# Attention and a mixture of experts on one core: stores placed one by one, and a rewritten order of attention's instructions

## Chip, core and metric

One core of a Trainium2 chip runs the whole program. The metric is the device time of one execution in microseconds, as a median of several runs. The core has five instruction queues that run beside each other: PE (TensorE, matmuls), DVE (VectorE), ACT (ScalarE), POOL (GpSimd) and SP (SyncE, which here only issues DMAs). Each runs its own list strictly in order and waits on semaphores for the others.

## What is computed

Sliding-window attention with four sink positions, and after it a mixture of eight experts with top-2 routing on the attention's output rows.

```python
B, H, S, D = 4, 8, 768, 64          # attention: batches, heads, tokens, head width
n_sink, window = 4, 128
scores = (q @ k.T) / sqrt(D)
keep = (pos_k < n_sink) | (0 <= pos_q - pos_k < window)
a = softmax(where(keep, scores, -1e9)); attn = a @ v
x = attn.transpose(0, 2, 1, 3).reshape(3072, 512)
noisy = x @ w_gate + log1p(exp(x @ w_noise)) * noise      # 8 experts
top2, weights = two largest of noisy, softmax of the two
for e in range(8):
    for k in range(2):
        out[mask] += weight * (relu(x[mask] @ w1[e]) @ w2[e])   # 512 -> 1024 -> 512
```

## The kernel before

**Two phases.** Phase one does attention, the routing of three of the four batches, and the first gathers and weight loads of expert 0. Phase two does the routing of the last batch and the eight experts. Phase one works in 48 steps n: 16 pairs of heads g, three steps each, n = 3 g + jj, four pairs to a batch. A step goes through the engines like this (the names are those of the functions in `attention`):

- `qk` (PE): scores of 256 query rows, tile S in a PSUM bank "D"; in the trace L403.
- `prev` and `cur` (ACT or DVE, then DVE): masked copy into the buffer `cbuf`; `mins` (DVE): row maxima `mn`; `minus_max` (POOL): `nb`.
- `exps_sums` (ACT): eight instructions of the softmax's exponentials with their sums.
- `ptr` (PE): the probabilities transposed into a "D" bank (L493); for odd steps `pcopy` (POOL or ACT) first lays the sinks' columns into `pcbuf`.
- `ptr_c` (ACT or DVE) copies them to the tile CT, `ptr_m` (DVE or POOL) makes the masked copy CM, `sink_c` the tile ps.
- `pv` (PE): output in a bank "X" (L519 with CT, L522 with CM), for odd steps `sinks` (PE, L534); `pv_c` (ACT or DVE) copies it to xtn and `rows` (DVE) turns it into token rows in the tile xr.

There are three "D" banks and two of "X", shared by all of these, by the gate's projections (`logits`: L734, L742), by the routing's matmuls and by the transposes of gathered rows (L1087).

**Token rows through memory.** `rows_d` stores a step's rows of a batch (four heads' pairs together) from xr to the buffer x_rows in memory, as four DMAs of 128 KB in rows of 512 bytes. `routing` ends for a batch with `keep`, four DMAs of 36 KB that lay the gate weights behind the rows, in pieces of 48 bytes. `gather` fetches 128 rows for an expert by an indirect DMA that POOL issues, once the rows and the weights of its batch have landed; `norm` (DVE, L1079), a transpose on PE and two copies follow.

**What sets the order.** Every step is announced to a planner (`Plan.op`, `Plan.dma`) with an engine, an estimated duration and what it reads and writes. For phase one `Plan.replay` then emits the steps in exactly the sequence of the table ORDER; a digit of SIDE for each step that can go to either of two engines says which, and a digit of BANKS for each use of a bank says which bank. A DMA announced with `Plan.dma` takes two entries of ORDER, one on SP and one for its transfer. For phase two `Plan.run` makes a list schedule from the estimates. The estimates are compiled into the order and are no measurement; the program that runs has only the order and the semaphores.

**Dummy matmuls.** 32 matmuls on constants (`warm`, L363) stand between the first blocks of PE.

## Time and profile before

| | |
|---|---|
| time, median of 3 runs (lowest, highest) | 742.03 us (740.33, 745.8) |
| the profiled execution: its own time | 741.34 us |
| its span on the core | 739.7 us |
| PE busy | 719.7 us, 97% of the span |
| DVE, ACT, POOL busy | 426.7, 328.6, 392.0 us |
| share of PE in the chain that ended last | 80% |
| first matmul of an expert's block on PE | 165.19 us |

A span of 739.7 us is what the trace shows of the execution; 1.6 us lie around it. Busy time on PE runs from a matmul's start to its modelled end, so that neighbours overlap. The idle time of PE is what can be read directly: it stands in brackets in the timeline, with what ended it.

### The profile page before, as it was taken

To read this page: it belongs to the slowest core of one execution; us is meant where nothing else is said; L and a number is where in the kernel's file an instruction comes from. 1 tells how busy PE (TensorE), PEld (TensorE's weight loads), DVE (VectorE), ACT (ScalarE), POOL (GpSimd) and SP (SyncE) were. 2 spreads that over 40 slices of the span, in tenths; PEclk is the share of its full clock that TensorE was granted. 3 is DMA by queue.
4 is the path that set the end of the run, shared out by engine and by line. 5 is a ranking of instruction groups with operands and counts; after the bars stand their busy time and mean duration, and the time that the engine had idled before them with its cause. 6 is when DMAs were issued, how large, how long until landed. Compare 5 with 4: busy or idle time off the path is not lost.

```text
span 739.7 us, 16786 instructions
## 1 busy us (share of the span) xinstructions
PE 719.7 (97%) x6531; PEld 622.6 (84%) x6531; DVE 426.7 (58%) x1105; ACT 328.6 (44%) x857; POOL 392.0 (53%) x613
## 2 busy tenths in 40 slices
PE   9999998989999999999999999999999999999995
PEld 5877776767888898899888988988889999998994
DVE  7889988888645555644465356536543654463320
ACT  5989998963233414332433234233413441433221
POOL 3645576761453757274727472847274564737212
PEclk9999999999999999999999999999999999999998
DMA  7548688648729626352645174516451662454033
GB/s 276 159 150 223 165 259 206 147 121 218 219 41 266 166 47 131 120 121 51 139 129 110 39 159 134 102 28 160 129 103 34 173 158 47 94 171 74 13 43 44
DMA packets 57634, 95.54 MB, mean 129 GB/s; under 512 B 19168, under 2 KB 32480, under 8 KB 57552
## 3 DMA queue, kind: packets, MB, share of 16 engines
q1 hardware_dynamic: 44240, 66.98, 30.5%
q0 software_dynamic: 13312, 27.46, 20.8%
q8 instruction: 52, 0.85, 0.5%
q14 instruction: 30, 0.25, 0.1%
HBM read 67.92 MB, written 26.50 MB: 128 GB/s over the span
## 4 chain that ended last, share of the span: by engine, by line
PE 80%; ACT 5%; issue 5%; DMA 4%; DVE 2%; POOL 2%; SPq 1%; POOLq 0%; ACTq 0%; DVEq 0%
PE H L1185 11%; PE H L1184 11%; PE H L1183 11%; PE Y L1250 11%; PE Y L1251 11%; PE Y L1249 10%; PE D L403 3%; PE D L493 3%; PE X L519 2%; ACT cbuf L446 2%; DMA st<-in_w1l 2%; PE X L522 2%; PE X L534 2%; POOL out L1273 2%; PE Y L1254 1%
## 5 line engine op out<-in xcount | busy, mean ns | idle before, releaser
L1034 POOL DMA_INDIRECT xg<-x_rows,rt_idq x173 | 174.3, 1008 | 59.6 <-issue 49.3
L1230 ACT ACTIVATE h<-H 128x384 fp32r<-128x384 f32 (+4 forms) x127 | 63.7, 501 | 258.8 <-PE H L1185 224.3
L1183 PE MATMUL H<-skn,w 128*128 128x384 f32 (+4 forms) x508 | 173.9, 342 | 0.0
L1184 PE MATMUL H<-sqn,w 128*128 128x384 f32 (+4 forms) x508 | 173.5, 342 | 0.4 <-DVE sqn L309 0.4
L1185 PE MATMUL H<-skn,w 128*128 128x384 f32 (+4 forms) x508 | 173.8, 342 | 0.0
L1238 DVE SCALAR_TENSOR_TENSOR h<-H,h 128x384 fp32r<-128x384 f32 (+4 forms) x167 | 74.9, 468 | 165.5 <-ACT h L1230 157.3
L1273 POOL DMA_INDIRECT out<-y,idx x53 | 94.0, 1774 | 50.8 <-ACT y L1258 34.3
L1282 POOL COPY spacer<-h 1x1 f32<-1x1 f32 x88 | 26.0, 296 | 145.7 <-ACT h L1230 144.3
L1184 PEld LDWEIGHTS H<-sqn,w 128*128 128x128 f32 x508 | 95.3, 188 | 7.0 <-DVE sqn L309 0.7
L1183 PEld LDWEIGHTS H<-skn,w 128*128 128x128 f32 x508 | 95.4, 188 | 6.8 <-DVE wc L1167 0.3
L1185 PEld LDWEIGHTS H<-skn,w 128*128 128x128 f32 x508 | 95.3, 188 | 1.6
L446 ACT ACTIVATE cbuf<-cbuf,nb 128x132 f32<-128x132 f32 x192 | 75.1, 399 | 2.5 <-POOL nb L435 2.2
L1251 PE MATMUL Y<-w2b,h 128*128 128x512 f32 x192 | 75.7, 394 | 0.0
L1251 PE MATMUL Y<-w2a,h 128*128 128x512 f32 x192 | 75.6, 394 | 0.0
L1250 PE MATMUL Y<-w2a,h 128*128 128x512 f32 x192 | 75.5, 393 | 0.0
L1250 PE MATMUL Y<-w2b,h 128*128 128x512 f32 x192 | 75.5, 393 | 0.0
L1249 PE MATMUL Y<-w2b,h 128*128 128x512 f32 x192 | 75.0, 391 | 0.0
L1249 PE MATMUL Y<-w2a,h 128*128 128x512 f32 x192 | 74.7, 389 | 0.0
L1101 ACT ACTIVATE skn<-xtn 128x512 fp32r<-128x512 f32 (+2 forms) x46 | 27.7, 602 | 54.1 <-DVE xtn L1092 51.0
L1171 DVE TENSOR_TENSOR gw<-xg,perm 32x8 f32<-32x8 f32 x173 | 27.2, 157 | 30.6 <-DMA xg<-x_rows,rt_idq 23.7
L403 PE MATMUL D<-kq 64*64 64x196 f32 (+3 forms) x832 | 40.2, 316 | 3.6 <-issue 1.3
L1251 PEld LDWEIGHTS Y<-w2b,h 128*128 128x128 f32 x192 | 36.0, 188 | 8.1 <-DVE h L1238 0.4
(214 smaller groups left out, 1212.4 us busy)
## 6 DMA issues: line engine op xcount, KB each, us to landing
st<-in_w1l SPq DMA_DIRECT2D x32, 512.0 KB
st<-in_w2l SPq DMA_DIRECT2D x32, 512.0 KB
kq<-in_kq SPq DMA_DIRECT2D x15, 792.0 KB
vn<-in_v SPq DMA_DIRECT2D x16, 384.0 KB
out<-zt SPq DMA_DIRECT2D x24, 256.0 KB
x_rows<-xr SPq DMA_DIRECT2D x48, 128.0 KB
xg<-x_rows,rt_idq POOLq DMA_INDIRECT x173
out<-y,idx POOLq DMA_INDIRECT x53
```

Of the source, the lines that this page charges most:

```text
L403: nc.tensor.matmul(x[:, o:o + w], kq(g)[r, 1, j, t], k[:, f:f + w], start=True, stop=True)
L446: nc.scalar.activation(C(n)[:, u], C(n)[:, u], AF.Exp, bias=get("nb", n)[:, u:u + 1], scale=1.0 / math.sqrt(D), accum_out=get("sm", n // 2 ...
L1034: nc.gpsimd.indirect_dma_start(out=x[:, i, :], out_offset=None, in_=xbuf.rearrange("r (q d) -> (r q) d", d=sh.SW), in_offset=bass.Indirect ...
L1183: nc.tensor.matmul(p, w[:, 0], xh, start=(i == 0), stop=False)
L1184: nc.tensor.matmul(p, w[:, 0], xl, start=False, stop=False)
L1185: nc.tensor.matmul(p, w[:, 1], xh, start=False, stop=(i == sh.DM // 128 - 1))
L1230: nc.scalar.activation(get("h", FC * q + f, [128, 2 * 128 * FIRST], F32R)[:, :width], H(q, f), AF.Relu)
L1238: nc.vector.scalar_tensor_tensor(h[:, o:o + s1 - s0], p[:, s0:s1], 0.0, h[:, s0:s1].bitcast(F32), op0=OP.max, op1=OP.subtract)
L1249: nc.tensor.matmul(p, hh, w[:, 0], start=(f == 0), stop=False)
L1250: nc.tensor.matmul(p, hh, w[:, 1], start=False, stop=False)
L1251: nc.tensor.matmul(p, hl, w[:, 0], start=False, stop=(f == FC - 1))
L1273: d = nc.gpsimd.indirect_dma_start(out=out, out_offset=bass.IndirectOffsetOnAxis(ap=c["idx"][:size(e, t), e, t:t + 1], axis=0), in_=get("y ...
```

## The change

Three things, in the planner's input and in its table.

- `rows_d` takes the quarter q as an argument and issues one DMA; the loop over the four quarters announces four entries to the planner where one stood before. `keep` is announced in the same way, one entry for each quarter, for the three batches of phase one. A gather names all the pieces that it needs.
- The estimates of many steps are other numbers, and those of a change between two kinds of PE blocks. A gather's rows are taken to be there 6.5 us after it, instead of 4.
- ORDER, SIDE and BANKS are new tables: 1,277 entries instead of 1,187, of which 90 are the 45 DMAs more that are counted one by one. The number of DMAs, their sizes and all the computing instructions are the same.

```diff
 ORDER = """
-0 1 8 10 4 5 12 14 16 18 20 22 9 13 24 26 28 30 15 32 2 3 6 7 34 36 17 25 38 27 23 40 118 119 19 42 44 46 21 48 89
+0 1 8 2 3 9 10 12 11 14 4 5 16 15 6 7 18 20 19 22 17 24 25 26 28 21 30 32 34 36 118 119 13 38 40 29 42 31 72 73 44
...
 SIDE = """
-11011100101010100110101010110001100010101000001100100010110010100010000010011000000000010101100100110100010000110000
+10011011001111101110100011101000110110100000101110001110110110010010000010000001001000001000101000010000110010010000
...
-                d = (d + (0 if self.ops[i][6] % 4 == kind % 4 else .2 if self.ops[i][6] == 1 else .15)) * (2 if t < self.cold else 1)
+                d = (d + (0 if self.ops[i][6] % 4 == kind % 4 else .1)) * (2 if t < self.cold else 1)
...
-    def rows_d(b, jj):
+    def rows_d(b, jj, q):
         x = get("xr", b * NJ + jj).rearrange("p a c s -> p a (c s)")
-        for q in range(4):
-            nc.sync.dma_start(dram(xbuf, (128 + b * S + jj * 256) * XW + q * sh.SW, [[XW, 32], [32 * XW, 8], [1, 128]]),
-                              x[32 * q:32 * q + 32])
+        nc.sync.dma_start(dram(xbuf, (128 + b * S + jj * 256) * XW + q * sh.SW, [[XW, 32], [32 * XW, 8], [1, 128]]),
+                          x[32 * q:32 * q + 32])
...
-            op("PE", .56 if odd else .45, n + .5 + P(g, "ptr"), lambda n=n: ptr(n), r=[("C", n)] + ([("pc", m)] if odd else []),
+            op("PE", .622 if odd else .505, n + .5 + P(g, "ptr"), lambda n=n: ptr(n), r=[("C", n)] + ([("pc", m)] if odd else []),
...
-                plan.dma(n + .7, lambda b=b, jj=jj: rows_d(b, jj), 2.2, r=[("xrp", n - NJ * i) for i in range(HP)],
-                         w=[("xrow", b * NJ + jj)], u=[("xr", b * NJ + jj)], n=4)
+                for q in range(4):
+                    plan.dma(n + .7, lambda b=b, jj=jj, q=q: rows_d(b, jj, q), .55, r=[("xrp", n - NJ * i) for i in range(HP)],
+                             w=[("xrow", b * NJ + jj, q)], u=[("xr", b * NJ + jj)])
...
-    plan.dma(z if last else plan.now, keep, 1.2 if last else 2.2, r=[t("w")], w=[("wrow", gid)], n=4 if last else 6.5)
+    if last:
+        plan.dma(z, keep, 1.2, r=[t("w")], w=[("wrow", gid)], n=4)
+    for q in range(0 if last else DM // 128):
+        plan.dma(plan.now, lambda q=q: keep((q,)), .55, r=[t("w")], w=[("wrow", gid, q)], n=1.62)
...
-        plan.op("Pool", 1.25, z, go, r=[("idg", b), ("wrow", b)] + [("xrow", i) for i in range(b * 3, b * 3 + 3)], w=[("xg", n)], lat=4 if t < sh.FA else 2.5)
+        plan.op("Pool", 1.25, z, go, r=[("idg", b), ("wrow", b)] + [("wrow", b, q) for q in range(4)] + [("xrow", i, q) for i in range(b * 3, b * 3 + 3) for q in range(4)], w=[("xg", n)], lat=6.5 if t < sh.FA else 2.5)
```

Three places of the order, before and after. Line numbers behind the tables are higher by 4 to 7 in the changed kernel.

SP's queue where the first batch's rows are stored (x_rows<-xr; kq and vn are the loads of queries, keys and values, out<-zt the zeroing of the output, vr the sinks' values), before:

```order
L377 DMA kq<-in_kq 128x1584 x2
L380 DMA vn<-in_v 128x768
L553 DMA x_rows<-xr 32x8x128 x4
L380 DMA vn<-in_v 128x768
L553 DMA x_rows<-xr 32x8x128 x4
L1427 DMA out<-zt 128x512
L553 DMA x_rows<-xr 32x8x128 x4
L377 DMA kq<-in_kq 128x1584
```

and after:

```order
L384 DMA vn<-in_v 128x768
L556 DMA x_rows<-xr 32x8x128
L381 DMA kq<-in_kq 128x1584
L556 DMA x_rows<-xr 32x8x128 x2
L384 DMA vn<-in_v 128x768
L381 DMA kq<-in_kq 128x1584
L556 DMA x_rows<-xr 32x8x128 x3
L384 DMA vn<-in_v 128x768
L556 DMA x_rows<-xr 32x8x128 x2
L381 DMA kq<-in_kq 128x1584
L556 DMA x_rows<-xr 32x8x128 x2
L381 DMA kq<-in_kq 128x1584
```

The twelve stores of the batch stood in three fours; now single ones, twos and threes stand between the loads.

POOL's queue at the first three gathers (xg<-x_rows; nb and sm are small steps of the softmax, w<-st a piece of a weight's split, CM<-CT the masked copy), before:

```order
L309 TENSOR_TENSOR dv<-vn 128x640
L309 TENSOR_TENSOR w_2679<-st,w_2679 128x256
L435 TENSOR_SCALAR nb<-mn 128x4
L459 TENSOR_SCALAR sm<-sm 128x8
L509 AFFINE_SELECT CM<-CT 128x256
L1028 DMA xg<-x_rows,idg 128x560 x3
L509 AFFINE_SELECT CM<-CT 128x512
```

and after:

```order
L313 TENSOR_TENSOR w_2599<-st,w_2599 128x256
L313 TENSOR_TENSOR dv<-vn 128x640
L439 TENSOR_SCALAR nb<-mn 128x4
L1035 DMA xg<-x_rows,idg 128x560
L513 AFFINE_SELECT CM<-CT 128x256
L1035 DMA xg<-x_rows,idg 128x560 x2
L439 TENSOR_SCALAR nb<-mn 128x4
```

The masked copy that stood ahead of all three gathers now stands behind the first.

PE's queue from a batch's last gate transposes (D<-idf,lt) to the first transposes of gathered rows (D<-idf,xg), before:

```order
L519 MATMUL X<-CT,vn 64x128 x4
L522 MATMUL X<-CM,dv 64x128 x2
L742 MATMUL D<-idf,lt 128x128 x2
L493 MATMUL D<-idf,cbuf 64x64 x16
L403 MATMUL D<-kq 64x196 x8
L519 MATMUL X<-CT,vn 64x128 x4
L522 MATMUL X<-CM,dv 64x128 x4
L1087 MATMUL D<-idf,xg 128x128 x4
```

and after:

```order
L746 MATMUL D<-idf,lt 128x128 x2
L497 MATMUL D<-idf,cbuf 64x64 x16
L497 MATMUL D<-idf,pcbuf 64x64 x4
L407 MATMUL D<-kq 64x196 x8
L497 MATMUL D<-idf,cbuf 64x64 x16
L523 MATMUL X<-CT,vn 64x128 x4
L526 MATMUL X<-CM,dv 64x128 x4
L538 MATMUL X<-ps,vr 128x128 x4
L1094 MATMUL D<-idf,xg 128x128 x4
```

Between the two there were a transpose block, a score block and a pv block; now two transpose blocks, a score block, a pv block and a sinks block.

## Rows read from the trace of the kernel before

**Rows 1.** Busy time by stretch (us, busy and instructions by engine; clock, DMA share, GB/s)

```profile
0.00:16.00 16.00, 14.22 (x180) 7.49 (x184) 10.97 (x36) 9.09 (x36) 5.29 (x22) 1.00 0.86 293
16.00:122.00 106.00, 102.17 (x2718) 83.10 (x2706) 92.82 (x276) 98.17 (x397) 63.93 (x158) 1.00 0.66 183
122.00:132.00 10.00, 7.71 (x142) 5.39 (x144) 7.35 (x18) 6.79 (x28) 6.62 (x13) 0.83 0.70 249
132.00:165.19 33.19, 29.58 (x680) 23.24 (x676) 28.20 (x89) 27.22 (x104) 22.51 (x45) 1.00 0.60 139
165.19:177.00 11.81, 11.13 (x50) 8.48 (x49) 8.39 (x45) 4.21 (x8) 0.00 (x0) 1.00 0.95 253
177.00:720.00 543.00, 542.63 (x2731) 485.05 (x2731) 278.97 (x646) 181.01 (x284) 288.92 (x372) 1.00 0.47 111
```

**Rows 2.** Waits of PE from 170 us on (us in total, times, longest)

```profile
PE X L848 <- DVE m L839: 0.7, 1, 0.7
```

**Rows 3.** Timeline of PE, start (start, us, instruction, idle before it)

```profile
9.88 2.17 PE L403 MATMUL D<-kq 64*64 64x196 f32 x52 [0.53 <-DMA kq<-in_kq]
```

**Rows 4.** Timeline of PE, pauses inside a block

```profile
65.19 0.64 PE L403 MATMUL D<-kq 64*64 64x132 f32 x16 [0.23 <-issue]
...
70.19 0.39 PE L403 MATMUL D<-kq 64*64 64x196 f32 x4 [1.03 <-issue]
...
96.85 0.49 PE L534 MATMUL X<-ps,vr 16*128 16x128 f32 x3 [0.92 <-issue]
...
154.29 0.33 PE L493 MATMUL D<-idf,cbuf 64*64 64x64 f32 x2 [0.49 <-issue]
```

**Rows 5.** Busy time by stretch, between two such pauses (columns as in rows 1)

```profile
65.17:70.18 5.01, 3.96 (x128) 3.13 (x127) 4.69 (x21) 4.74 (x18) 4.13 (x11) 1.00 0.96 265
...
96.84:101.39 4.55, 4.31 (x128) 3.52 (x128) 2.69 (x21) 3.80 (x12) 2.71 (x12) 1.00 0.88 227
```

**Rows 6.** Timeline of SP's DMA queue (start, us of issuing)

```profile
66.78 3.34 SPq L553 DMA_DIRECT2D x_rows<-xr  x4
...
94.79 6.04 SPq L553 DMA_DIRECT2D x_rows<-xr  x8
...
113.08 2.61 SPq L874 DMA_DIRECT2D x_rows<-rt_w  x4
```

**Rows 7.** Timeline of PE, 126 to 134 us

```profile
126.29 0.43 PE L522 MATMUL X<-CM,dv 128*64 128x128 f32 x2 [0.38 <-issue]
127.03 0.38 PE L742 MATMUL D<-idf,lt 128*128 128x128 f32 x2 [0.31 <-issue]
128.72 1.13 PE L493 MATMUL D<-idf,cbuf 64*64 64x64 f32 x32 [1.31 <-ACT ps L526]
129.63 1.53 PE L403 MATMUL D<-kq 64*64 64x196 f32 x16
...
133.68 0.89 PE L403 MATMUL D<-kq 64*64 64x196 f32 x16
```

**Rows 8.** Timeline of PE, blocks without a wait

```profile
27.30 0.85 PE L403 MATMUL D<-kq 64*64 64x196 f32 x16
28.08 0.66 PE L519 MATMUL X<-CT,vn 128*64 128x128 f32 x8
...
35.48 0.85 PE L403 MATMUL D<-kq 64*64 64x196 f32 x16
36.15 0.64 PE L493 MATMUL D<-idf,cbuf 64*64 64x64 f32 x32
```

**Rows 9.** Groups of ACT's instructions, 0 to 170 us (count, busy us, mean ns, idle)

```profile
L409 ACT ACTIVATE CT<-D 128x512 f32<-128x512 f32 x45 | 26.5, 591 | 5.1 <-PE D L742 2.4 <-DVE CM L506 1.6 <-PE D L493 0.7
```

**Rows 10.** Timeline of POOL, then of DVE, at the first gather

```profile
123.43 1.23 POOL L1028 DMA_INDIRECT xg<-x_rows,idg  x1 [0.71 <-DVE mn L432]
...
129.89 0.72 DVE L1079 TENSOR_TENSOR xg<-xg 128x512 f32<-128x512 f32 x1
```

**Rows 11.** Chain of waits, 108 to 136 us (start, us, what)

```profile
114.38 5.27 DMA x_rows<-rt_w
```

More of the change, by code (lines that the diff above doesn't have):

```diff
@@ L591, in attention @@
             need = {jj, max(jj - 1, 0)}
-            op("PE", .68 if jj else .61, n + P(g, "qk"), lambda n=n: qk(n), r=[("kq", g, i) for i in need], w=[("S", n)],
+            op("PE", .66 if jj else .555, n + P(g, "qk"), lambda n=n: qk(n), r=[("kq", g, i) for i in need], w=[("S", n)],
                u=[("kq", g), ("C", n)], kind=3)
-            op("ACT", .46 if jj else .27, n + P(g, "prev"), lambda n=n, e=0: prev(n, e), r=[("S", n)], w=[("C", n, 0)], u=[("C", n)],
-               alt=("DVE", .61 if jj else .34, 0))
+            op("ACT", .5 if jj else .28, n + P(g, "prev"), lambda n=n, e=0: prev(n, e), r=[("S", n)], w=[("C", n, 0)], u=[("C", n)],
+               alt=("DVE", .69 if jj else .36, 0))
             if not jj:
@@ L621, in attention @@
                 pe = ("Pool", "ACT", "DVE")[PR.get("pc_eng", 0)]
-                op(pe, {"Pool": .45, "ACT": .3, "DVE": .2}[pe], n + .5 + P(g, "pcopy"), lambda m=m, e=0: pcopy(m, e), r=cs, w=[("pc", m)],
-                   alt=("ACT", .3, 0))
-            op("PE", .56 if odd else .45, n + .5 + P(g, "ptr"), lambda n=n: ptr(n), r=[("C", n)] + ([("pc", m)] if odd else []),
+                op(pe, {"Pool": .53, "ACT": .47, "DVE": .2}[pe], n + .5 + P(g, "pcopy"), lambda m=m, e=0: pcopy(m, e), r=cs, w=[("pc", m)],
+                   alt=("ACT", .47, 0))
+            op("PE", .622 if odd else .505, n + .5 + P(g, "ptr"), lambda n=n: ptr(n), r=[("C", n)] + ([("pc", m)] if odd else []),
                w=[("P", n)], kind=3)
@@ L870, in routing, with keep @@
     aux(lambda: s_.tensor_copy(rt("w")[:, :, 1, :E], rt("w")[:, :, 0, :E]), [], ["w"])
-    def keep():
-        for q in range(DM // 128):
+    def keep(qs=range(DM // 128)):
+        for q in qs:
             nc.sync.dma_start(dram(xbuf, (T0 + 1) * 128 * sh.XW + q * sh.SW + 128, [[sh.XW, 128], [128 * sh.XW, nt], [1, E + C]]),
                               rt("w")[:, :, q // 2, :])
-    plan.dma(z if last else plan.now, keep, 1.2 if last else 2.2, r=[t("w")], w=[("wrow", gid)], n=4 if last else 6.5)
+    if last:
+        plan.dma(z, keep, 1.2, r=[t("w")], w=[("wrow", gid)], n=4)
+    for q in range(0 if last else DM // 128):
+        plan.dma(plan.now, lambda q=q: keep((q,)), .55, r=[t("w")], w=[("wrow", gid, q)], n=1.62)
     most = c["most"]
```

28 lines of the change are left out of this document (14 added, 14 removed), and 86 rows, old and new, of the table ORDER.

## Prediction

> **What bounds the kernel now.** I read the stretches first, then the waits of PE, then its timeline, then the queues that feed it. Before 16 us PE is busy 14.22 of 16.00 us; from 16 to 165.19 us it idles 3.83, 2.29 and 3.61 us in the three stretches, 9.73 us together; from 177 to 720 us it is busy 542.63 of 543.00 us [rows 1]. So PE is the bound nearly everywhere, and phase two cannot move: PE's blocks stand in the same order there in both programs, and its one wait at the start, 0.7 us for the routing's mask [rows 2], keeps its place between the same blocks. Whatever the change does to the time, it does by moving the moment at which PE is done with attention, 165.19 us. In the long middle stretch ACT is busy 98.17 and DVE 92.82 of 106.00 us against PE's 102.17 [rows 1]: three engines with little room, so an order that feeds PE badly shows at once, and one that feeds it perfectly can win no more than PE's idle time and what its clock and its changes between kinds of blocks cost.
>
> Where that idle time lies is the whole question. Six of PE's pauses, 0.23, 1.03, 0.92, 0.24, 0.35 and 0.49 us, 3.26 us together, stand inside a block whose other matmuls had already begun, and the profile names no engine; the first, the last and the two longest are shown [rows 4]. Between neighbours of them PE issues 128 matmuls and 127 or 128 weight loads, 256 instructions [rows 5], and the others are multiples of that apart. I take them for waits for the next page of PE's own program, which a DMA brings. Three more pauses, 0.38, 0.31 and 1.31 us, stand together from 126 to 129 us, and after them the granted clock is down: the stretch's mean is 0.83 of full [rows 1], and a score block takes 1.53 us instead of 0.89 [rows 7]. The rest, 9.73 - 3.26 - 2.00 = 4.47 us, are short waits for ACT or DVE spread over the phase.
>
> **The change, term by term.** *Computing.* No instruction is added or taken away, and the sizes of the DMAs are the same; SP issues 45 entries more on paper and the same DMAs in fact. Cost: nothing.
>
> *The start.* PE waits 0.53 us for the second load of keys [rows 3]. Two of the 32 dummies that stood behind that score block now stand ahead of it, and fill the wait; later PE has them no more to do. Bounds 0.53 us and nothing; I take -0.3.
>
> *Changes between kinds of blocks.* A score block followed by pv takes 28.08 - 27.30 = 0.78 us to the next block's start, one followed by a transpose 36.15 - 35.48 = 0.67 [rows 8]: 0.11 us for the change of kind. Along PE's order up to phase two I count 127 changes before and 121 after. 6 x 0.11 = 0.7 us; between nothing and twice that, since other pairs differ. I take -0.7.
>
> *Stores one by one, and the program's pages.* Four of the six page pauses (0.23, 1.03, 0.92, 0.24, 2.42 us) fall during or just behind runs of row stores, such as four from 66.78 and eight from 94.79 us [rows 6], with DMA engines 0.96 and 0.88 busy [rows 5]. In the new order the first batch's stores go out in ones, twos and threes. But SP does not wait for a planned time, only for data, so where several stand in a row (sevens and fives in the later batches) they go out together as before. I take 0.4 of the 2.42 us, -1.0. Bounds: all 3.26 us gone, or 1.5 us more, as much as the two pauses at 70 and 154 us, if the stores now meet other fetches. [...]
>
> *The pause at 126 us and the clock.* Here 2.00 us of idling and the slow blocks behind it come together; 0.17 x 10 = 1.7 us of full-speed time are lost to the clock, of which PE used most: I take 1.4. Sum 3.4 us [rows 1, 7]. Three gathers, three zeroing stores and two small loads fall on the DMA engines at once there. In the new order the zeroing stores are apart from each other, a masked copy stands between the first gather and the next two, and PE has five blocks instead of three between the gate's transposes and the first gathered rows. The rows of the first gather were used 129.89 - 123.43 = 6.46 us after it [rows 10], and DVE did not wait for them, so more distance wins nothing there by itself; what can go is the crowding. I take two thirds of 3.4 us, -2.2; bounds -3.4 and nothing.
>
> *The other short waits, 4.47 us.* For each of 203 blocks of PE I counted how many steps of the engines the order goes on from the last step of another engine that feeds it or frees its bank to the block itself. At most four: 49 before, 36 after; twelve or more: 63 before, 91 after. Exactly one: 1 before, 10 after. Most inputs are earlier, a few are at the last moment. ACT loses nine instructions net, three of them copies of 0.591 us [rows 9], so 1.8 us at least and 5.3 us at most of its load, and DVE takes five: relief where it is tightest (ACT 0.93 busy, DVE 0.88), and it is not PE's time. By the count 4.47 x 13 / 49 = 1.2 us go; for the ten close ones I take half back, -0.6. Bounds -4.47 and +3, two pauses of 1.31 with a little clock.
>
> *The queues passed.* The weights' stores of the second batch (`keep`) now stand 13 entries of the order ahead of the first gather instead of 32; what this may cost is the third rival. POOL takes four of the `pcopy` instructions from ACT; it is busy 63.93 of 106.00 us [rows 1], which hides them.
>
> **Sum.** -0.3 - 0.7 - 1.0 - 2.2 - 0.6 = -4.8 us, 741.34 - 4.8 = 736.5 us for the profiled execution. The median of the runs lies 0.7 us above it, so 737.2 us. All lower bounds together give -13.1, all upper ones +4.5; they do not come together.
>
> **The rivals.** *The pauses only move.* The planner knows neither the pages nor the clock, and these two are 3.26 + 3.4 of the idle and slow time. If new places take their part and the ten close inputs eat the rest, only start and kinds remain: 742.03 - 1.0 = 741 us. For it: SP still runs its stores back to back, and the pauses come every so many of 256 instructions whatever stands there. Against: both tend to follow crowded DMA engines, and the crowding is less in the two places shown.
>
> *Nearly all of it goes.* A PE that waits for nothing from 16 us on but half its pages would win 0.3 + 0.7 + 1.6 + 3.4 + 3.5 = 9.5 us: 732.5 us. For it: PE is the fullest engine, and the distances grew. Against: ACT and DVE at 0.9 leave little to absorb a late step.
>
> *POOL held by the first gather: slower.* One store of weights needed 5.27 us from issue to landing [rows 11], and SP some 0.65 us to issue each of the four [rows 6]. With 13 of 1,277 entries over 165 us the last one is planned 1.7 us ahead of the gather. SP is normally early: the data of these stores is ready 77 entries, 10 us, ahead of the gather, and issuing and landing take 2.6 + 5.3 = 7.9 us. If SP comes to them more than 2.1 us late, POOL waits at the gather, and behind it stand `nb`, for which ACT's exponentials wait, and then PE's transposes. If SP keeps only to the planned time, that is 0.65 + 5.27 - 1.7 = 4.2 us of POOL, and 1.7 us of clock if PE stops: +5.9 in place of the -2.2 above, so 742.03 - 2.6 + 5.9 = 745 us, slower than before.
>
> **How the numbers follow.** The forecast 0.50, its own range 735 to 740; pauses only move 0.24, 740 to 744; nearly all goes 0.18, 731 to 735; POOL held 0.08, 743 to 750. For 8 in 10 I reach from 732 to 743.5. One per cent, 7.4 us, is about what a measurement can tell from no change: below 734.6 lie most of the second rival and the forecast's tail, 0.21; above 749.5 the worst of the third, 0.04; the rest, 0.75, is within it.
>
> **What would show it.** The first L1190 matmul of the expert's block near 160.5 us instead of 165.19, and everything behind it as far apart as now. Page pauses below 3 us in sum; no drop of the clock between 120 and 135 us; PE idle between 16 us and that matmul near 6.8 us; no pause of POOL ahead of the first gather on a store. I am wrong if that matmul is where it was with the same idle sum (first rival), if phase two has a new wait of PE, or if a stop of PE follows the first gather.

## The result: slower by 0.7%, and the profile after

Over 20 runs of each the changed kernel takes 749.26 us at the median (744.95 to 754.35) and the kernel before 744.0 (740.33 to 746.25): a ratio of 1.0073, with an interval of 1.0052 to 1.0095. A second measurement beside other runs gave 1.0100 (1.0075 to 1.0125). The forecast was 737.2 us, the range ended at 743.5, and the sign is wrong. By the bound of 1% named there the first measurement is "within 1%"; but both intervals lie above 1.

The profiled execution after took 748.19 us, with a span of 746.5. The first group is busy time by stretch, with the columns of [rows 1], from 0 us to the end of PE's work; the third stretch after the start is the one that the forecast aimed at, the two last are only 3.4 us long.

```profile
0.00:16.00 16.00, 14.75 (x179) 7.90 (x182) 11.22 (x36) 7.51 (x29) 5.74 (x21) 1.00 0.86 295
16.00:122.00 106.00, 99.57 (x2620) 81.62 (x2614) 89.31 (x265) 91.61 (x372) 59.98 (x155) 0.98 0.61 178
122.00:132.00 10.00, 9.02 (x203) 6.26 (x200) 8.70 (x26) 9.94 (x45) 7.61 (x13) 1.00 0.91 234
132.00:171.49 39.49, 33.28 (x726) 25.21 (x719) 34.08 (x101) 28.95 (x109) 24.28 (x55) 0.96 0.64 141
...
184.00:727.00 543.00, 542.75 (x2732) 485.30 (x2732) 279.00 (x646) 181.02 (x284) 288.56 (x372) 1.00 0.47 112
16.00:171.49 155.49, 141.87 (x3536) 113.08 (x3529) 132.09 (x390) 130.50 (x524) 91.86 (x220) 0.98 0.64 172
68.46:71.87 3.41, 3.41 (x52) 2.85 (x45) 1.38 (x6) 1.74 (x6) 2.17 (x6) 0.50 0.83 210
153.80:157.20 3.40, 3.40 (x45) 2.51 (x49) 1.63 (x4) 2.40 (x9) 3.28 (x4) 0.50 1.08 112
```

The first L1190 matmul of the expert's block (L1183 in the kernel before) stands at 171.49 us instead of 165.19, and phase two takes what it took: 542.75 us busy in 543 here, 542.63 in [rows 1]. So 6.30 of the 6.85 us by which the profiled execution is longer lie ahead of that matmul. The row of before for the same whole is this (16 us to the first L1190 matmul):

```profile
16.00:165.19 149.19, 139.46 (x3536) 111.73 (x3524) 128.37 (x381) 132.18 (x527) 93.07 (x214) 0.99 0.65 178
```

PE executes 3,536 recorded matmuls in both. It is idle for 155.49 - 141.87 = 13.62 us instead of 9.73, and busy 2.41 us longer: 3.89 + 2.41 = 6.30 us. Most of what it is longer busy goes with the clock: one stretch of 3.41 us at half clock more is 1.7 us, an estimate from its length and clock. Two stretches of 3.41 us at a granted clock of 0.50 stand in the trace after ahead of that matmul; before there was one such stretch, at 128.41 us, behind the pause of [rows 7]. That place is better now: from 122 to 132 us PE now is busy 9.02 us at a clock of 1.00, against 7.71 at 0.83. The two new places are elsewhere, and the timeline of PE shows what stands just ahead of each:

```profile
67.74 0.63 PE L497 MATMUL D<-idf,cbuf 64*64 64x64 f32 x27 [1.35 <-issue]
...
75.59 0.29 PE L497 MATMUL D<-idf,cbuf 64*64 64x64 f32 x5 [1.96 <-issue]
...
147.25 0.57 PE L497 MATMUL D<-idf,cbuf 64*64 64x64 f32 x21 [0.41 <-issue]
...
153.72 0.35 PE L497 MATMUL D<-idf,cbuf 64*64 64x64 f32 x3 [1.77 <-issue]
```

These are page pauses as in [rows 4]: inside a block, with no engine named, a multiple of 256 instructions of PE apart. Six of them, 0.13, 0.15, 1.35, 1.96, 0.41 and 1.77 us, come to 5.77 us where [rows 4] had 3.26. The pauses of 1.35 and 1.77 us are followed within 0.8 us by half clock, the one of 1.96 is not. The other idle time grew as well, from 6.47 to 7.85 us, with these in it (timeline, and the waits of PE from 130 us on):

```profile
136.22 0.66 PE L1094 MATMUL D<-idf,xg 128*128 128x128 f32 x4 [0.91 <-DVE xg L1086]
139.01 0.63 PE L1094 MATMUL D<-idf,xg 128*128 128x128 f32 x4 [1.31 <-issue]
```

```profile
PE X L852 <- DVE m L843: 1.7, 1, 1.7
```

So, of the 6.30 us: page pauses +2.51, other idle time +1.38, PE's busy time +2.41. The rest of the difference, some 0.5 us, lies behind that matmul, where phase two's wait for the routing's mask is 1.7 us here and 0.7 in [rows 2].

A second trace of the changed kernel (**after0** below; 747.98 us) is as long and divides the loss otherwise. The first group is its stretch from 16 us to the first L1190 matmul, the second two waits of PE:

```profile
16.00:171.76 155.76, 142.37 (x3531) 114.42 (x3520) 132.11 (x390) 130.49 (x524) 92.22 (x220) 0.97 0.62 172
```

```profile
67.95 0.78 PE L497 MATMUL D<-idf,cbuf 64*64 64x64 f32 x27 [1.61 <-issue]
...
139.22 0.63 PE L1094 MATMUL D<-idf,xg 128*128 128x128 f32 x4 [1.86 <-ACT cbuf L450]
```

Its page pauses, 0.50, 1.61, 0.52, 0.12, 0.36 and 0.25 us, come to 3.36 us, hardly more than in the kernel before, and three stretches of 3.41 us are at half clock, from 68.29, 139.97 and 160.45 us. Of its 6.57 us page pauses are +0.10, other idle time +3.56 and PE's busy time +2.91. What both traces have in common is 3.7 to 3.9 us more of idling and more time at half clock; how much of the idling is page pauses differs from one execution to the next.

### The profile page after: what moved, and what is told of

It reads as the page before. It is cut to its first block, busy times and chain, and to the rows that moved or that the text cites. A ratio compares the mean times of both kernels' runs of the same rounds, so it can differ in the third digit from the quotient of the medians.

```text
span 746.5 us, 16776 instructions
## 1 busy us (share of the span) xinstructions
PE 722.1 (97%) x6531; PEld 624.5 (84%) x6531; DVE 430.0 (58%) x1110; ACT 325.2 (44%) x848; POOL 390.9 (52%) x617
## 3 DMA queue, kind: packets, MB, share of 16 engines
q1 hardware_dynamic: 44240, 66.98, 30.5%
## 4 chain that ended last, share of the span: by engine, by line
PE 80%; issue 5%; ACT 4%; DMA 4%; POOL 3%; DVE 3%; SPq 0%; POOLq 0%; ACTq 0%; DVEq 0%
PE H L1192 11%; PE H L1191 11%; PE H L1190 11%; PE Y L1257 10%; PE Y L1258 10%; PE Y L1256 10%; PE D L407 3%; PE D L497 3%; PE X L523 2%; ACT cbuf L450 2%; POOL out L1280 2%; DMA st<-in_w1l 1%; PE X L526 1%; PE X L367 1%; PE X L538 1%
## 5 line engine op out<-in xcount | busy, mean ns | idle before, releaser
L1190 PE MATMUL H<-skn,w 128*128 128x384 f32 (+4 forms) x508 | 173.8, 342 | 0.0
L1190 PEld LDWEIGHTS H<-skn,w 128*128 128x128 f32 x508 | 95.4, 188 | 6.5
L1258 PEld LDWEIGHTS Y<-w2a,h 128*128 128x128 f32 x192 | 36.0, 188 | 7.7
```

Source lines behind the costliest of these rows:

```text
L1190: nc.tensor.matmul(p, w[:, 0], xh, start=(i == 0), stop=False)
L1258: nc.tensor.matmul(p, hl, w[:, 0], start=False, stop=(f == FC - 1))
```

## What a page pause waits for

Each page of PE's program, 256 matmuls and weight loads, comes as one packet of 16 KB on a queue of its own: the profile calls q8 "instruction" and counts 52 packets and 0.85 MB on it before and after, and 6,531 matmuls and as many weight loads make 51 times 256. Reading the trace's packets against the matmuls, up to the expert's first, shows three things. A page's packet starts behind PE's entry into the page before, by 0.1 to 5.4 us where PE does not wait for another engine at the entry itself. It can stand behind data that SP has issued: the one for the entry at 61.28 us starts at 65.23, just as a load of keys issued at 59.35 has landed (65.22). It does not wait for all of it: the packet of 73.17 has landed at 74.10, a load of keys issued at 67.16 only at 75.80. And where PE has paused it goes on 1.4 to 1.6 us after the packet has landed. PE takes 4 to 5.5 us for a page without a wait, which leaves a packet some 2 us, an estimate from these figures: the least delay behind a pause of [rows 4] is 2.13 us, while one of 2.65 us, behind the entry at 115.75 of the changed kernel, brought no pause.

Here is the pause of 1.96 us. PE enters a page at 67.74 us. SP's timeline shows what was issued just ahead: a load of keys of 792 KB half a microsecond before, with stores of rows around it.

```profile
65.14 0.36 SPq L384 DMA_DIRECT2D vn<-in_v  x1
65.55 1.57 SPq L556 DMA_DIRECT2D x_rows<-xr  x2
67.16 0.46 SPq L381 DMA_DIRECT2D kq<-in_kq  x1
67.67 1.12 SPq L556 DMA_DIRECT2D x_rows<-xr  x2
```

The view of the DMA queues (packets, MB, share of 16 engines) from that entry to 73.10 us has this one row, so that no program was fetched in 5.4 us:

```profile
q1 hardware_dynamic: 1057, 1.30, 84.8%
```

The same view from 73.10 to 75.59 us has the packet:

```profile
q1 hardware_dynamic: 190, 0.11, 15.9%
q8 instruction: 1, 0.02, 2.3%
```

The other two long pauses look the same: entry at 61.28 us with a load of keys issued at 59.35, packet 3.96 us later, pause 1.35; entry at 147.25 with a load of 512 KB of an expert's second matrix (st<-in_w2l) issued at 146.12 behind a run of row stores and gate weights, packet 3.96 us later, pause 1.77. In the second trace the same three loads stand ahead of the same entries, and the pauses are 1.61, 0.52 and 0.25 us. In the kernel before the six pauses of [rows 4] follow packets that start 2.13 to 3.97 us after the entry. The rows of [rows 6] were read there as the cause, and the row stores are part of what is queued, but a load of keys weighs six times as much as one of them.

## The experiments

All compare with the kernel before, run beside them on the same chip; ratios are to it, with the interval. The first set asks which part is the loss: the places of a few DMAs against PE's pages, SP's order, the order of the computing, or the page grid.

**hold3**: the changed kernel, with three DMAs held until PE has entered the page in question: the two loads of keys above behind the transposes of steps 17 and 19, and the 512 KB load of an expert's second matrix behind those of step 42.

```diff
+HOLD = {654: 421, 722: 457, 1262: 1066}
...
+                if i in HOLD:
+                    self.tc.add_manual_dep(last_[i], last_[HOLD[i]].name, mybir.DependencyInfo(
+                        mybir.DependencyClass.Sync, mybir.DependencyReason.DATA), reason="hold")
```

> The changed kernel, with three DMAs held back until a named block of PE has run: the keys of pair 9 (issued at 59.35 us before), the keys of pair 10 (67.16 us) and the second matrix's piece of expert 0 (146.12 us). Each stood some 0.6 to 2 us ahead of the moment at which PE entered a new 256th instruction (61.28, 67.74, 147.25 us), and the next page of PE's program was then fetched 4.0, 5.4 and 4.0 us later. Nothing else is moved. Theory A (the fetch stands in line behind data that SP issued ahead of it): the fetches come under 3 us after the entry, the page pauses of 1.35, 1.96 and 1.77 us fall to under 0.8 us together, the clock stays up at 68 and 154 us, and the time is 5 to 8 us shorter than the changed kernel's 749.3, so 741 to 744 us. Theory B (the new order of the computing steps is the loss, and the pauses are only where it shows): the same waits reappear on other engines' steps, 748 to 751 us.

Measured: 744.1 us, 1.0036 (1.0013 to 1.0059). The two pauses at 67.74 and 75.59 us and the one at 153.72 are gone. The entry that belongs to the pause above is at 65.46 us here, and SP issues the keys only behind it; the second of these groups is the DMA view from 66.35 to 69.50 us, and the packet is in it, 0.95 us after the entry by its record. The third is the timeline of PE:

```profile
64.92 1.02 SPq L565 DMA_DIRECT2D x_rows<-xr  x2
66.35 0.36 SPq L390 DMA_DIRECT2D kq<-in_kq  x1
66.75 1.68 SPq L565 DMA_DIRECT2D x_rows<-xr  x2
```

```profile
q1 hardware_dynamic: 787, 1.01, 107.0%
q8 instruction: 1, 0.02, 2.3%
```

```profile
69.15 0.69 PE L506 MATMUL D<-idf,cbuf 64*64 64x64 f32 x32
69.67 0.85 PE L416 MATMUL D<-kq 64*64 64x196 f32 x16
```

The DMA engines are no less busy than in the changed kernel (1.07 of the nominal share), and PE goes through. So at this entry it is the place of the load that decides, not the amount of traffic. Page pauses of 0.72, 0.50, 0.40 and 0.52 us stand elsewhere, the first two at the next two pages. The expert's first matmul is at 167.51 us, 3.98 us earlier than after and 2.32 later than before. The row up to it:

```profile
16.00:167.51 151.51, 138.64 (x3540) 110.73 (x3529) 131.72 (x390) 130.45 (x524) 92.50 (x220) 0.99 0.63 177
```

PE idles 12.87 us, only 0.75 less than in the first trace of the changed kernel: 3.6 us of page pauses are gone and 2.9 us of other waits have come. What fell is its busy time, by 3.23 us; half clock is granted once (3.41 us from 160.68) instead of twice. The runs say the same: the median granted clock is 0.9935 here and 0.996 in the repeat hold3b, 0.994 and 0.995 in the kernel before beside them; it is 0.9915 and 0.992 in the two measurements of the changed kernel, with 0.9965 in the kernel before beside the second.

**sp_before** and **sp_after**: the kernel before with the new stores and SP's new order, and the changed kernel with SP's old order (ORDER's entries on SP put in the other's sequence, nothing else on PE, ACT, DVE or POOL).

> The changed kernel's computing order, sides and banks, with SP's queue in the sequence of the kernel before (row stores and the routing's stores in fours, zeroing and loads where they stood). Theory A: the page pauses are set by what SP issues just ahead of PE's page entries, so they change altogether: below 4 us in sum instead of 5.8, no pair of pauses over 1 us, 743 to 747 us. Theory B: the computing order decides, 748 to 751 us.

> The computing order, sides and banks of the kernel before, with SP's queue in the sequence of the changed kernel (one row store stands one place earlier, since a copy on DVE would else wait for it in a circle). Theory A: the queue brings its long runs along, but PE's page entries stand elsewhere against it, so the page pauses are not those of the kernel before: 745 to 750 us. Theory B: the old computing order keeps its time, 743 to 745 us.

Measured: 750.2 us, 1.0126 (1.009 to 1.0163), and 751.93 us, 1.015 (1.0109 to 1.019). Both crossings are as slow as the changed kernel or slower. The losses are new ones: in the first PE waits 3.5 us for a masked copy, in the second 3.61 (waits, then timeline of PE), and PE runs at half clock for 10.2 and 13.6 us ahead of phase two.

```profile
PE D L497 <- ACT cbuf L450: 3.5, 1, 3.5
```

```profile
115.19 1.26 PE L407 MATMUL D<-kq 64*64 64x196 f32 x12 [3.61 <-DVE cbuf L429]
```

In the first the page pauses come to 3.0 us, fewer than in the changed kernel's first trace, and the time is no shorter. So exchanging one order shows what a misfit costs rather than the share of either.

**split2** and **before_split2**: each dummy split in two, so that every page of PE begins 64 instructions earlier in the program, in the changed kernel and in the kernel before.

```diff
-        nc.tensor.matmul(get("X", first, [128, 4, 128], F32, "ps"), one, one[:, None, :].to_broadcast([128, 4, 128]),
-                         start=True, stop=True)
+        for i in range(2):
+            nc.tensor.matmul(get("X", first, [128, 4, 128], F32, "ps")[:, i * 2:(i + 1) * 2], one,
+                             one[:, None, :].to_broadcast([128, 2, 128]), start=True, stop=True)
```

> The changed kernel with each of the 32 dummy matmuls of 512 columns done as two of 256: the same columns, 64 instructions more ahead of everything, so that every page of PE's program is entered 64 instructions (1.2 us) earlier in the work. Nothing of the real work is moved. Theory A: the page pauses change places; those behind the entries at 67.74 and 147.25 us go, since the long run of SP's DMAs is then behind the entry and not ahead of it, and others come; their sum differs from 5.8 us by over 1.5 us and the time by over 1.5 us, most likely down to 745 to 748 us. Theory B: the pauses stay at the same steps of the work and the time at 749 to 750 us.

> The kernel before with each dummy matmul done as two of half the columns: PE enters every page 64 instructions (1.2 us) earlier in the work. The same edit made the changed kernel 5 us longer. If the kernel before has page entries that happen to stand well against SP's queue, it loses too: 742 to 747 us, with a page pause over 1.5 us or more half-clock stretches. If its queue is robust, 740 to 741 us.

Measured: 752.97 us, 1.0168 (1.0121 to 1.0215), and 741.52 us, 1.0011 (0.9981 to 1.0042). With the grid moved the changed kernel has its longest pause at another place, where the packet starts 4.54 us after an entry at 60.74 us:

```profile
67.70 0.54 PE L527 MATMUL X<-CM,dv 128*64 128x128 f32 x5 [3.37 <-issue]
```

The kernel before gets pauses of 1.96 us at 65.57 and 1.91 at 111.27 and is level all the same: no half clock follows them. So the pauses move with the grid in both kernels. In split2 half clock follows 1.2 us behind, for 6.83 us. That a pause costs time where the clock falls, or where PE would not have waited for another engine soon after, fits these runs and is not shown.

**early_kq**: the kernel before, with one load of keys issued ahead of eight row stores instead of behind them; SP's queue:

```order
-L553 DMA x_rows<-xr 32x8x128 x4
-L1427 DMA out<-zt 128x512
-L553 DMA x_rows<-xr 32x8x128 x4
-L377 DMA kq<-in_kq 128x1584
+L377 DMA kq<-in_kq 128x1584
+L553 DMA x_rows<-xr 32x8x128 x4
+L1427 DMA out<-zt 128x512
+L553 DMA x_rows<-xr 32x8x128 x4
```

> The kernel before, with one load issued earlier: the keys of pair 10 (792 KB), at 70.17 us behind eight row stores, now go out ahead of those, near 64 us, a microsecond before PE enters a page at 65.2 us. Nothing else is moved. Theory A: it makes in the kernel before what hold3 took out of the changed one. The fetch after that entry, 2.1 us late before, is over 4 us late, the pause at 70.19 us grows from 1.03 to some 3 us and the clock falls behind it: 2 to 5 us longer than the kernel before. Theory B (the computing order): no change, within 1 us.

Measured: 745.37 us, 1.0041 (1.0006 to 1.0075). This makes the fault in a kernel that did not have it. The load goes out at 64.29 us, PE enters a page at 65.77, and the DMA view up to 69.90 us has no packet of q8; PE then pauses at the next entry. SP, then DMA queues from 65.77 to 69.90 us, then PE:

```profile
64.29 0.43 SPq L377 DMA_DIRECT2D kq<-in_kq  x1
64.82 2.59 SPq L553 DMA_DIRECT2D x_rows<-xr  x4
```

```profile
q1 hardware_dynamic: 721, 1.29, 101.9%
```

```profile
72.41 0.39 PE L403 MATMUL D<-kq 64*64 64x196 f32 x4 [2.68 <-issue]
```

Where the kernel before paused 1.03 us [rows 4] it now pauses 2.68, and others follow later (1.15, 2.25 and 1.00 us). Up to the expert's first matmul, at 168.99 us, PE idles 14.62 us instead of 9.73, with one stretch at half clock as before. None of the bytes changed. The loss is small: its interval begins at 0.06%.

**before_hold**: the kernel before, with two loads of keys held behind the entries ahead of its pauses of 0.92 and 0.35 us.

```diff
+HOLD = {887: 626, 981: 696}
```

> The kernel before with two loads held for the block of PE at a page's entry: the keys of pair 13 (90.30 us, entry at 91.52, fetch 3.0 us later, pause 0.92 us) and of pair 14 (103.26 us, entry at 105.73, fetch 3.1 us later, pause 0.35 us). Theory A: both pauses go, 0.5 to 2 us below the kernel before, which is at the edge of what the runs can tell; a ratio of 0.997 to 1.000. Theory B: no change.

Measured: 740.96 us, 0.9994 (0.9961 to 1.0027). The two pauses go (packets at 0.73 and 1.72 us instead of 2.99 and 3.08), but one of 0.98 us comes one page later, behind an entry at 95.94 whose packet starts after 2.81 us. Nothing is won: the held load (92.98 us), one of weights and one of values now stand ahead of the next entry.

**joined** and **late**: the changed kernel with its stores of rows and the routing's stores joined again in fours, and hold3 with five other loads held as well, the second of hold3's held longer, and the keys of pairs 10 to 13 later in SP's queue.

```order
-L556 DMA x_rows<-xr 32x8x128
-L381 DMA kq<-in_kq 128x1584
-L556 DMA x_rows<-xr 32x8x128 x2
-L384 DMA vn<-in_v 128x768
-L381 DMA kq<-in_kq 128x1584
-L556 DMA x_rows<-xr 32x8x128 x3
-L384 DMA vn<-in_v 128x768
-L556 DMA x_rows<-xr 32x8x128 x2
-L381 DMA kq<-in_kq 128x1584
-L556 DMA x_rows<-xr 32x8x128 x2
-L381 DMA kq<-in_kq 128x1584
-L556 DMA x_rows<-xr 32x8x128 x2
+L556 DMA x_rows<-xr 32x8x128 x4
+L381 DMA kq<-in_kq 128x1584
+L556 DMA x_rows<-xr 32x8x128 x4
```

```diff
-HOLD = {654: 421, 722: 457, 1262: 1066}
+HOLD = {654: 421, 722: 644, 603: 530, 800: 567, 900: 668, 953: 716, 1053: 738, 1262: 1066}
```

> The changed kernel with its row stores and the routing's stores joined again in fours, each four where its first stood in SP's queue; loads, zeroing and all computing as in the changed kernel. If storing one by one is itself the loss, 740 to 743 us on this scale (the changed kernel 747.6, the kernel before 740.5). Theory A: the stores as such are neither good nor bad, only what stands ahead of a page entry counts, and that is drawn anew: the page pauses stand elsewhere, 744 to 751 us. Theory B: 747 to 748 us.

> The changed kernel with SP's queue thinned where PE enters a page. The keys of pairs 10 to 13 go out later, up to 16 us (they were loaded up to 23 us ahead of their first use), and six key and value loads and the second matrix's piece wait, as in hold3, for the block of PE at a page's entry, so that the page's fetch stands ahead of them. The computing order is untouched. Theory A (fetches in line behind data): page pauses of PE between 16 and 165 us under 1.5 us in sum (5.8 in the changed kernel, 2.1 in hold3), and 2 to 4 us below hold3's ratio if nothing else is woken: a ratio to the kernel before of 0.996 to 1.002. Theory B (the new computing order itself is the loss): the pauses go and the time does not, a ratio of 1.003 to 1.008 as hold3 and the changed kernel have it.

Measured: 750.6 us, 1.0121 (1.0074 to 1.0168), and 749.19 us, 1.0118 (1.0092 to 1.0143). Joining does not help, so that the stores are single is not what costs here. In the second my holds went too far: page pauses fell to 1.11, 0.32 and 0.29 us, but the values of a later pair came too late, and half clock for 6.83 us followed:

```profile
113.38 0.66 PE L532 MATMUL X<-CT,vn 128*64 128x128 f32 x8 [2.29 <-DMA vn<-in_v]
```

In sum the page pauses are 2.5 us in joined and 1.7 in late, below the kernel before's 3.26, and both are slower than it by over 1%. So that sum alone does not order the times.

**noload_before** and **noload_after**: both kernels without the later loads of keys, queries and values and without the code at the end that takes up experts' overflow, which leaves the order of the computing with less than half the traffic of this phase; **after0** is the changed kernel again, and **noload_after2** a repeat. The loads left out come to 16 MB (66.98 against 50.93 MB on the queue q1), not 18.

```diff
-        return get("kq", g, [128, 2, NB, KW])
+        return get("kq", g % 3, [128, 2, NB, KW])
...
-        plan.dma((g - 1) * NJ + PR.get("load_v", 1) if g else -16, lambda: load_v(g), 1.45, w=[("vn", g)])
+        plan.dma((g - 1) * NJ + PR.get("load_v", 1) if g else -16, (lambda: load_v(g)) if g < 2 else lambda: None, 1.45, w=[("vn", g)])
```

> The changed kernel without the loads of keys for pairs 3 to 15 and of values for pairs 2 to 15 (18 MB; their buffers keep the first pairs' numbers, so the output is wrong) and without the code at the end that takes up experts' overflow. All computing stands as before in the same order. Both theories: PE's page fetches start under 2 us after the entry and page pauses are under 0.5 us in sum. Theory A: with the loads away the new computing order shows what it is worth, 1 to 4 us shorter than the order of the kernel before without the same loads. Theory B: 3 us or more longer than that.

> The kernel before without the same loads and without the overflow code (output wrong). The pair to the run above, which see: theory A has this one 1 to 4 us longer than it, theory B 3 us or more shorter. Against the kernel before itself: its page pauses of 3.3 us go and perhaps the slow clock at 128 us, 2 to 6 us shorter.

> The changed kernel itself, beside the others on the same chip: a ratio of 1.005 to 1.009 to the kernel before, as first measured (1.0073). If pauses on pages are a matter of where DMAs happen to stand, its page pauses stand at the same entries as in the first trace (67.74, 75.59 and 153.72 us), give or take one; theory B says nothing on that.

> The run it is compared with, noload_after again on the same chip: 739.8 us first time, a ratio of 0.999. Both theories: the same again within 1 us.

Measured: 739.8 us, 0.9992 (0.9974 to 1.001), against 737.6 us, 0.9956 (0.9936 to 0.9977); after0 747.62 us; noload_after2 738.95 us, 0.9962 (0.9942 to 0.9982). Side by side on one chip the new order without loads is slower by 2.2 us: all its twelve runs (739.14 us and more) are longer than all twelve of the other (738.64 and less). The repeat, on another chip and without noload_before beside it, is level with it by the ratios, within the intervals. The rows from 16 us to the first L1190 matmul, of before and of after without loads:

```profile
16.00:158.85 142.85, 134.94 (x3481) 107.99 (x3480) 125.22 (x380) 130.51 (x525) 94.21 (x214) 1.00 0.33 77
```

```profile
16.00:162.49 146.49, 135.26 (x3489) 108.46 (x3480) 132.62 (x390) 129.43 (x523) 91.74 (x218) 1.00 0.34 78
```

PE is busy 134.94 and 135.26 us at full clock: the changes between kinds of blocks, by which I had 0.7 us less, do not show. It idles 7.91 and 11.23 us: the new order makes PE wait 3.3 us more when the clock plays no part and no page pause is over 0.1 us; in noload_after2 it is 2.9 us more (10.81). DVE is busy 7.4 us longer. One piece of this stands at the same blocks with and without loads, here in the first trace of the changed kernel:

```profile
39.60 0.90 PE L407 MATMUL D<-kq 64*64 64x196 f32 x16 [0.46 <-ACT CT L413]
...
44.60 0.64 PE L738 MATMUL D<-xtn,wbd 128*32 128x256 f32 x8 [0.37 <-DVE CM L510]
...
46.66 0.52 PE L497 MATMUL D<-idf,cbuf 64*64 64x64 f32 x20 [0.40 <-DVE CM L510]
```

These three are 1.23 us, 1.25 in noload_after and in hold3; the kernel before waits 0.20 and 0.30 us in this stretch.

**noload_close** and **hold3_close**: nine small blocks of PE (gate, routing, gathered rows) moved one place back, without loads and with hold3's holds, since the new order has ten blocks right behind their last input.

```order
+L523 MATMUL X<-CT,vn 64x128 x4
+L526 MATMUL X<-CM,dv 64x128 x4
 L738 MATMUL D<-xtn,wbd 32x256 x4
-L523 MATMUL X<-CT,vn 64x128 x4
-L526 MATMUL X<-CM,dv 64x128 x4
```

> The changed kernel without the loads of keys (pairs 3 to 15) and values (pairs 2 to 15) and without the overflow code (output wrong), and with nine small blocks of PE moved one place back, behind the block that followed them: two of the gate's projections ahead of pv(10) and pv(23), one ahead of pv(47), transposes of the gate (two) and of gathered rows (two), a rank and a placement. In the same run without the moves PE waits 4.7 us in front of these nine. Theory C (the new computing order loses by small blocks that stand directly behind what feeds them): 1.5 to 4 us shorter than that run, so at or below the old order without loads. Theory D (PE waits there because ACT and DVE are full; whoever is moved, the wait comes back at the next block): within 0.7 us of it.

> hold3 (the changed kernel with three DMAs held for a page's entry), with the nine small blocks moved back as well. Theory C: the two causes add up, 1.5 to 4 us below hold3's 744.1, at 740 to 742.5 us, level with the kernel before. Theory D: hold3's time. The pages are entered at other blocks here and there, so a new collision may hide part of it.

> hold3 again, beside hold3_close on the same chip: a ratio to the kernel before of 1.001 to 1.006 (1.0036 first time).

Measured: 739.53 us, 0.9966 (0.9943 to 0.9989), beside noload_after2's 738.95; and 743.17 us, 1.0013 (0.999 to 1.0037), beside 742.84 us, 1.0016 (0.9992 to 1.004), for **hold3b**, which is hold3 once more. Placing the small blocks later wins no time in either. In the trace without loads PE does idle less, 9.19 us against 10.81 in noload_after2, but a stretch of 3.41 us at half clock (from 133.93) stands there and none in the other. So that close inputs cost the rest is not shown.

**noload_dv** and **hold3_dv**: POOL's differences of the values (`dv`, 1.55 us) in five pieces, so that a small instruction of DVE stands beside a piece of some 0.4 us (2.11 us for the five).

```diff
-        minus(nc.gpsimd if eng == "Pool" else nc.vector, get("dv", g, [128, 2, NB - 1, D]), x[:, :, 1:, :], x[:, :, :NB - 1, :])
+        y = get("dv", g, [128, 2, NB - 1, D])
+        for i in range(NB - 1):
+            minus(nc.gpsimd, y[:, :, i], x[:, :, i + 1], x[:, :, i])
```

> The changed kernel without the loads of keys (pairs 3 to 15) and values (pairs 2 to 15) and without the overflow code (output wrong), with POOL's difference of the values, 16 instructions of 1.6 us, done in five pieces each, so that an instruction of DVE that stands back for POOL does so for some 0.4 us at most. Theory E (the new order puts three of the routing's small DVE steps beside dv, and DVE holds PE up by it): no DVE step of 0.2 us takes over 0.7, and the time is 1 to 3 us below noload_after's, a ratio to the kernel before of 0.993 to 0.996. Theory D (ACT and DVE are full anyway): the same time within 1 us, or up to 1 us more for POOL's extra instructions.

> hold3 with POOL's difference of the values in five pieces as well. Theory E: 1 to 3 us below hold3's ratio of 1.002 to 1.004, so level with the kernel before. Theory D: hold3's ratio.

Measured: 737.49 us, 0.9943 (0.9915 to 0.9972), and 743.24 us, 1.003 (1.0 to 1.006). What this was aimed at is there: in noload_after2 a routing step of DVE with 12 columns takes 1.52 us, up to 141.39, and POOL's instruction ends at 141.35; with the pieces it takes 0.43. DVE and POOL of noload_after2, then both of noload_dv:

```profile
139.87 1.52 DVE L925 TENSOR_SCALAR rt_vl<-r 128x12 f32<-128x12 f32 x1
...
139.80 1.55 POOL L313 TENSOR_TENSOR dv<-vn 128x640 f32<-128x640 f32 x1
```

```profile
139.89 0.43 DVE L927 TENSOR_SCALAR rt_vl<-r 128x12 f32<-128x12 f32 x1
...
139.84 2.11 POOL L313 TENSOR_TENSOR dv<-vn 128x128 f32<-128x128 f32 x5
```

The 1.4 us (by the ratios) by which noload_dv lies below noload_after2 agree in size with the 0.8 us by which its first L1190 matmul is earlier (161.69 against 162.51), but the intervals overlap and the two were not run side by side; with the loads there is no gain at all. So this is a possible part of the rest, and not shown as one.

## Why the prediction was wrong

**What bounds the kernel.** Right: PE, and only the moment at which it is done with attention. Phase two kept its length, but its one wait did not "keep its place" at 0.7 us; it became 1.7 us, since the mask is later relative to PE; some 0.5 us shows in the span of the first trace.

**Stores one by one, and the program's pages: the step that failed.** It took -1.0 us with bounds of -3.26 and +1.5. The pauses rose by 2.51 us in the first trace, beyond the bound, with half clock close behind two of them, and by 0.10 us in the second, with half clock behind one; and by the holds the places of three DMAs cost 4.5 us, three times the upper bound. The reading of the pauses as waits for PE's program was right, and so was the place of the cause, crowded DMA engines. But I saw the row stores next to the pauses and took what changes for them as what changes the pauses. At the three entries it is a large load issued in the last two microseconds before PE enters a page: hold3 moves only three such loads and takes the ratio from 1.0073 and 1.0100 to 1.0036 and 1.0016, by the means 0.61%, 4.5 us; early_kq moves one load the other way in the kernel before and loses 0.41%. It is no rule for every entry: the keys issued at 104.81 us in the changed kernel, 1.64 us ahead of the entry that the count of 256 puts at 106.45, brought no pause. Rows for it lay in the trace of before: its pause of 0.92 us has a load of keys issued at 90.30 us, 1.23 us ahead of an entry. I counted the pages only between pauses [rows 5] and did not put the new order's loads on the new grid. The new order of PE and SP can't be read for times, so this would have given a wider bound, not the place of each pause. Most crossings cost nothing in either order: of the 28 entries into a page between 16 us and the expert's first matmul six have a pause before and six after, of up to 1.03 and 1.96 us; split2 has one of 3.37.

**The pause at 126 us and the clock.** The slow clock is gone from 122 to 132 us, and PE idles 0.98 us there instead of 2.29; in the second trace it is still 1.93. But the term counted the gain of a place and not the loss of the whole. PE stops behind that place instead, 0.91 and 1.31 us ahead of gathered rows in the first trace, 0.40 and 1.86 in the second, where half clock follows at 139.97 us. And the clock fell twice elsewhere, 3.41 us each at half, so that about 1.7 us of full-speed time are lost more than before, and 3.4 in the second trace, where I had two thirds of 1.4 fewer. Nor do the loads make the wait: in noload_before PE waits 2.48 us there for the same copy of ACT, at full clock. The whole is the first rival's mechanism ("new places take their part"), to which I gave 0.24, with a range that ended at 744 us. It should have had a losing side.

**The other short waits.** Wrong in sign: -0.6 with bounds to +3; without loads PE idles 3.3 and 2.9 us more in the new order, about the upper bound, and with them idle time other than page pauses, the place at 126 us included, rose by 1.38 and 3.56 us. The count of steps between a block and its last input improved and said nothing of time, because steps are of very different length, and one and the same step of DVE (`rt_vl`) took 0.17 us in one batch and 1.52 in another, beside POOL's `dv`, in the trace after. Moving nine of the ten close blocks won no time (noload_close). The waits at 39 to 47 us make some 0.7 us of the rise; the rest was not settled, and DVE behind POOL's `dv` fits in size only.

**The start and the changes of kind.** PE is busy 14.75 us before 16 us instead of 14.22, with one matmul fewer on record there, so nothing of 0.3 us can be seen in the end; and 0.7 us for kinds do not show in PE's busy time without loads (+0.32). Both terms were too small to matter.

**POOL held by the first gather** did not happen, though the sign named with it, a stop of PE behind the first gather, is there (1.31 us up to 139.01). The gather waits 1.85 us for its indices and not for a store:

```profile
127.31 1.23 POOL L1035 DMA_INDIRECT xg<-x_rows,idg  x1 [1.85 <-DVE ids L1017]
```

So the loss has two parts. About 4.5 us go with the places of three DMAs, shown by moving them in the changed kernel. (Both kernels were measured twice, each time beside the kernel before and not beside each other.) That these DMAs make the pauses at their three entries is shown by the traces with and without the holds, and by early_kq in the other kernel. How a pause becomes time is not: by the holds the first pair of traces has 0.75 us less idling and 3.23 less busy time, the second (after0 and hold3b) 3.49 and 2.02, and joined and late have few page pauses and are as slow as the changed kernel. The rest, 1.2 to 2.7 us by the two measurements of the held kernel, is what is left with the new order of the computing; without loads that order is slower by 2.2 us side by side. Which waits make it up is open for the most part. In the held kernel part of it stands at POOL's copy behind the gathers (0.53 us in the changed kernel without holds):

```profile
159.22 0.34 PE L506 MATMUL D<-idf,pcbuf 64*64 64x64 f32 x6 [1.76 <-POOL pcbuf L496]
```

None of the versions with all loads beat the kernel before; hold3b, hold3_close, before_hold and before_split2 are level with it within their intervals.

## What to carry to other kernels

When a program streams its instructions from memory, mark the entries into pages on the timeline of the fullest engine, and look what large DMA was issued in the two microseconds before each: a load of 792 KB there can cost a pause one page later (1.35 and 1.96 us here), and the same load issued just behind the entry let that fetch through, though it may stand in the way of the next. Take two traces of a kernel before dividing a loss of some microseconds: here page pauses were 5.77 us in one and 3.36 in the other. A change of order moves both the pages and the DMAs, so a pause that a new order removes at one place is to be priced together with what it may make at the others, upwards as well as down. A count in steps of the order is no measure of slack; only durations are.

## What the runs showed of the hardware

- Where PE has paused for a page it goes on 1.4 to 1.6 us after the packet has landed; a packet takes 0.9 to 1.8 us in the traces before and after up to the expert's first matmul. Together that is 2.3 us at the least, about half of the 4 to 5.5 us of a page.
- The granted clock falls to 0.50 for 3.41 us (for 6.83 in split2 and late) behind some pauses (1.35 and 1.77 us in the changed kernel, 2.25 in early_kq, 3.37 in split2, a wait of 2.29 for values in late) and not behind others (1.96 in the changed kernel, 2.68 in early_kq, 1.96 and 1.91 in before_split2, 2.48 in noload_before). What tells them apart was not found.
- Between runs of one kernel the time follows the mean granted clock: over 39 runs of the kernel before by 0.70 us for each 0.001, over all 125 beside the experiments by 0.78. The medians of the clock are 0.996 before and 0.9915 after, which by that slope goes with some 3 of the 5.3 us; whether the clock makes the time or pauses make both, this does not say.
- The routing's step `rt_vl` of DVE, 128x12, takes 1.52 us where POOL's `dv` runs beside it, up to 141.39 us in noload_after2 and 148.45 in the trace after, where `dv` ends at 141.35 and 148.42. In another batch of the trace after it takes 0.17 us, and beside the pieces of `dv` in noload_dv 0.43. What holds it no run shows.
